# Reordering the first loads of a fused attention and bilinear kernel: key weights in pieces ahead of the second token tile

## The chip, the cores and the metric

The kernel runs on one core of a Trainium2 chip. The metric is device time in microseconds (us), lower being better. Each kernel ran several times. A profile is one execution recorded instruction by instruction; its "span" is some 1.7 us shorter than the time listed for the same execution (1436.2 against 1437.96 us). Times within a profile count from the start of the span.

## The reference, cut to what matters

Four layers run in sequence on x of 2048 tokens by 1024 features: linear attention (A), a bilinear feed-forward block (B), then A and B again with the same weights.

```
x = A_x
x = x + _A_ref(_layernorm(x), A_wqkv, A_wo)              # first the projections q, k of the normalised x
x = x + _B_ref(_layernorm(x), B_w_gate, B_w_up, B_w_down)
x = x + _A_ref(_layernorm(x), A_wqkv, A_wo)
x = x + _B_ref(_layernorm(x), B_w_gate, B_w_up, B_w_down)
```

Only the first microseconds of the first A are changed. A token tile is 128 tokens. It is loaded, normalised, transposed by TensorE so that features lie on partitions, and multiplied by the key weights, 1024 x 1024, in two halves of 512 columns. I number the tiles from one in the text; the code counts from zero.

## The kernel before

Every operation goes through a small planner that records what it reads and writes and derives the semaphore waits from that. The parts that matter here:

```
            def proj(kind, i, h, mid=None):          # tile i, column half h: eight matmuls
                ...
                for ks in ((range(0, 4), range(4, 8)) if mid else (range(KT),)):
                    P.add("pe", ... [e.matmul(psb(bank), xnT[:, k, ...], t[:, k, h * 512:(h + 1) * 512], ...) for k in ks] ...,
                          rd=r_xT(i * 128, (i + 1) * 128) + r_w(base, h * 512, (h + 1) * 512), pwr=[bank])
                    if mid: mid(); mid = None          # something put between the two groups of four
    ...
            lead = [[lambda: lnp.start(2), lambda: lnp.step_t(1)], [lambda: lnp.b_one()], ...]   # after each projection
            #        statistics of tile three, transposes of tile two
    ...
        dma(x_res[:, 0, 0:dh0], ...); dma(x_res[:, 0, dh0:D], ...)    # tile one, two halves
        xload(1)                                                     # tile two
        load_w("k", 0); load_w("k", 1)                               # key weights, 1 MB each
        xload(2); load_w("q", 0); xload(3); load_w("q", 1); xload(4); xload(5)
```

`start` makes a tile's statistics, `b_one` normalises it, and `step_t` makes TensorE transpose it and ScalarE copy the result. All loads are issued by the sync engine (SP).

## Time and profile before

| | before |
|---|---|
| time, median of 3 runs | 1436.02 us (1435.92 to 1436.86) |
| profiled execution, span | 1436.2 us |
| TensorE busy | 1421.7 us, 99% |
| TensorE idle before the first projection | 2.85 us |
| first key half, issued and landed | 2.2 and 9.7 us |
| granted TensorE clock at half | 7.6 to 14.5 us |

A timeline line reads: start, duration, engine, source line, operation, tiles, count, and in brackets the idle time before it with what ended it. The lines themselves are in the prediction.

### The profile page before, as it was taken

The numbers are of one execution on the slowest core, as the hardware profiler recorded it, in microseconds if no ns is written. First come the engines' busy times: TensorE is split into PE (matmuls) and PEld (weight loads), VectorE is DVE, ScalarE is ACT, GpSimd is POOL, SyncE is SP. The second block draws the span as 40 slices with busy tenths as digits, with TensorE's granted clock in tenths as the row PEclk, the third lists the DMA queues.
The fourth block names the chain that finished last, engine by engine and source line by source line (L and its number), as shares of the span: only waits on it lengthen the run. The fifth ranks groups of instructions, "written<-read, shape, count | busy, mean of one in ns | idle before, by whom it ended". The sixth has DMA issues, their size and how long they took to land.

```text
span 1436.2 us, 21761 instructions
## 1 busy us (share of the span) xinstructions
PE 1421.7 (99%) x8110; PEld 787.9 (55%) x8170; DVE 1212.8 (84%) x2377; ACT 677.0 (47%) x1386; POOL 148.5 (10%) x176
## 2 busy tenths in 40 slices
PE   8999999999999999999999999999999999999999
PEld 3444444555545566664544444446666475666547
DVE  6987878999978799988779978778888887888888
ACT  4573355444410266662157824567776004777400
POOL 2202621000010000002000045310000100000000
PEclk9999999999999999999999999999999999999999
DMA  6778978997786777768883266767775976777653
GB/s 195 165 212 224 214 172 195 298 303 267 257 268 203 249 248 251 257 241 286 245 272 109 88 164 158 191 174 262 257 251 192 289 256 224 259 262 256 207 192 120
DMA packets 272570, 320.73 MB, mean 223 GB/s; under 512 B 164048, under 2 KB 214992, under 8 KB 272464
## 3 DMA queue, kind: packets, MB, share of 16 engines
q1 hardware_dynamic: 272464, 319.34, 72.6%
q8 instruction: 64, 1.05, 0.3%
q14 instruction: 42, 0.34, 0.1%
HBM read 236.45 MB, written 73.40 MB: 216 GB/s over the span
## 4 chain that ended last, share of the span: by engine, by line
PE 94%; DVE 4%; issue 1%; ACT 1%; DMA 0%; POOL 0%; DVEq 0%
PE ps L1357 28%; PE ps L1774 17%; PE ps L1438 17%; PE ps L1173 8%; PE ps L1275 7%; PE ps L907 6%; PE ps L939 6%; PE ps L1692 5%; DVE arena L777 2%; DVE arena L452 1%; PE ps L1199 1%; DVE arena L780 0%; PE ps L1226 0%; DVE arena L959 0%; DVE arena L624 0%
## 5 line engine op out<-in xcount | busy, mean ns | idle before, releaser
L777 DVE TENSOR_TENSOR arena<-arena 128x512 f16<-128x512 f16 (+9 forms) x1015 | 497.8, 518 | 59.5 <-ACT arena L1442 34.2
L1357 PE MATMUL ps<-arena 128*128 128x512 f16 x1888 | 457.1, 379 | 1.0 <-DVE arena L780 1.0
L780 DVE SCALAR_TENSOR_TENSOR arena<-ps,arena 128x512 f16<-128x512 f32 (+3 forms) x545 | 353.9, 664 | 68.7 <-PE ps L1774 28.4
L1438 PE MATMUL ps<-arena 128*128 128x256 f16 x2184 | 287.5, 273 | 1.0 <-DVE ps L1451 1.0
L1357 PEld LDWEIGHTS ps<-arena 128*128 128x128 f16 (+1 forms) x1888 | 182.9, 98 | 163.6 <-ACT ps L1386 3.8
L1438 PEld LDWEIGHTS ps<-arena 128*128 128x128 f16 (+1 forms) x2184 | 212.2, 98 | 91.6 <-ACT arena L1442 6.9
L1774 PE MATMUL ps<-arena 128*128 128x512 bf16 (+1 forms) x1102 | 242.6, 379 | 0.9
L1774 PEld LDWEIGHTS ps<-arena 128*128 128x128 f16 x1120 | 109.6, 98 | 130.2
L1362 ACT ACTIVATE arena<-ps 128x512 f32<-128x512 f32 x224 | 133.8, 597 | 76.3 <-PE ps L1357 61.5
L1442 ACT ACTIVATE arena<-ps 128x256 f32<-128x256 f32 x351 | 125.1, 384 | 26.9 <-PE ps L1438 22.0
L939 PE MATMUL ps<-arena 128*128 128x512 f16 (+1 forms) x551 | 122.2, 379 | 1.0 <-ACT arena L946 0.4
L1173 PE MATMUL ps<-arena 128*128 128x512 bf16 x498 | 114.7, 379 | 0.7
L1275 PE MATMUL ps<-arena 128*128 128x512 bf16 x502 | 110.3, 379 | 0.5
L457 POOL TENSOR_SCALAR arena<-arena 128x1 f32<-128x1 f32 x64 | 24.8, 388 | 818.0 <-DVE arena L456 818.0
L1448 ACT COPY ps<-ps 128x256 f32<-128x256 f32 x182 | 66.3, 364 | 74.8 <-DVE arena L780 29.3
L1386 ACT COPY ps<-ps 128x512 f32<-128x512 f32 x112 | 65.4, 584 | 64.4 <-PE ps L1357 52.2
L1041 POOL TENSOR_TENSOR arena<-arena 128x1024 f16<-128x1024 f32 x32 | 77.2, 2412 | 158.3 <-DVE arena L1039 147.8
L452 DVE BATCH_NORM_STATS2 arena<-arena 128x6 f32<-128x512 bf16 x128 | 88.1, 688 | 5.5 <-DMA arena<-in_A_x_dram 3.1
L939 PEld LDWEIGHTS ps<-arena 128*128 128x128 f16 x560 | 54.0, 98 | 68.2 <-ACT arena L946 5.7
L907 PE MATMUL ps<-arena 128*128 128x512 bf16 x375 | 86.1, 385 | 3.6 <-DVE arena L474 2.8
L1692 PE MATMUL ps<-arena 128*128 128x256 f16 (+1 forms) x784 | 86.8, 273 | 0.2 <-ACT ps L1705 0.2
L1451 DVE TENSOR_TENSOR ps<-ps,arena 128x256 f32<-128x256 f32 x182 | 76.7, 428 | 10.5 <-PE ps L1438 9.6
(62 smaller groups left out, 901.3 us busy)
## 6 DMA issues: line engine op xcount, KB each, us to landing
arena<-w_scratch SPq DMA_DIRECT2D x84, 896.0 KB, 4.5
arena<-t_scratch SPq DMA_DIRECT2D x32, 896.0 KB, 6.0
arena<-in_B_w_down_dram SPq DMA_DIRECT2D x24, 896.0 KB, 5.0
arena<-sp_scratch SPq DMA_DIRECT2D x26, 768.0 KB, 4.3
w_scratch<-arena SPq DMA_DIRECT2D x28, 512.0 KB, 6.2
arena<-w_scratch SPq DMA_DIRECT2D x28, 384.0 KB, 5.2
x_scratch<-arena SPq DMA_DIRECT2D x40, 256.0 KB, 7.2
arena<-x_scratch SPq DMA_DIRECT2D x40, 256.0 KB, 5.6
```

The lines of the kernel that those rows point to most:

```text
L777: P.add("dve", lambda e: e.tensor_tensor(out=out, in0=a, in1=b, op=op), rd=rd, wr=wr, prd=prd)
L780: P.add("dve", lambda e: e.scalar_tensor_tensor(out=out, in0=a, scalar=sc, in1=b, op0=ALU.mult, op1=op1), rd=rd, wr=wr, prd=prd)
L907: P.add("pe", (lambda ks: lambda e: [e.matmul(psb(bank), xnT[:, k, i * 128:(i + 1) * 128], t[:, k, h * 512:(h + 1) * 512], start=(k == 0), ...
L939: P.add("pe", lambda e: [e.matmul(psb(bank), a[0][:, k, :], b[0][:, k, :], start=(q in (1, 5) and k == 0), stop=(k == 3), skip_group_check ...
L1173: return [e.matmul(psb(bank), xrt[t][:, jj * 128:(jj + 1) * 128], pk[:, h, t, :], start=(t == tok[0]), stop=(t == tok[NST - 1])) for t in ts]
L1275: return [e.matmul(psb(bank), xnT[:, g, i * 128:(i + 1) * 128], wp[:, g, dh * 512:(dh + 1) * 512], start=(dh == 0 and g == 0), stop=(g == ...
L1357: P.add("pe", lambda e: [e.matmul(psb(bank), w[:, k, :], x[:, k, :], start=(start and k == 0), stop=(k == 3), skip_group_check=True) for k ...
L1362: P.add("act", lambda e: e.activation(t, psb(bank), AF.Copy, scale=SG), prd=[bank], wr=r)
L1438: P.add("pe", lambda e: [e.matmul(psb(bank)[:, 256 * half:256 * half + 256], w[:, k, :], xx[:, k, :], start=(start and k == 0), stop=(k == ...
L1442: P.add("act", lambda e: e.activation(d, src, AF.Copy, scale=sc), prd=[xk], wr=rd_)
L1692: P.add("pe", lambda e: [e.matmul(psb(bank)[:, 256 * half:256 * half + 256], a[:, k, 128 * r:128 * r + 128], b[:, k, :], start=(start and ...
L1774: P.add("pe", lambda e: [e.matmul(psb(bank), hv[:, 7 * hf + k, t * 128:(t + 1) * 128], w[:, k, :], start=(q in "15" and hf == 0 and k == 0 ...
```

## The change

The intent is to start the first projection as soon as tile one is ready: its weights come ahead of tile two, in two pieces of 512 KB, so that the first four matmuls need only the first piece. Tile two's transposes move into the middle of the second projection, since tile two now comes later; tile three's already stood in the middle of the fourth. The diff, cut to its core (the removal of the half-started statistics is left out):

```
-                          rd=r_xT(...) + r_w(base, h * 512, (h + 1) * 512), pwr=[bank])
+                          rd=r_xT(...) + r_w(base, h * 512, (h + 1) * 512)[ks[0]:ks[-1] + 1], pwr=[bank])
...
-                j1 = lnp.start_half()
                 lnp.b_one()
                 lnp.step_t(1)
-                lnp.start_rest(j1)
+                lnp.start(1)
...
+            mids = {("k", 0, 0): lambda: None, ("k", 0, 1): lambda: lnp.step_t(1), ("k", 1, 1): lambda: lnp.step_t(1)}
-            lead = [[lambda: lnp.start(2), lambda: lnp.step_t(1)], ...
+            lead = [[lambda: lnp.start(2)], ...
...
+        for hf in range(2):
+            dma(wk[:, 4 * hf:4 * hf + 4, 0:512], wqkv_v[:, 4 * hf:4 * hf + 4, D:D + 512], ..., (KW["k"][0], KKB)[hf])
         xload(1)
-        load_w("k", 0)
         load_w("k", 1)
```

More of the change, by code (lines that the diff above doesn't have):

```diff
@@ L292, in build_kernel @@
     KXB = dkey("x0b")
+    KKB = dkey("k0b")
     KXS = [dkey("xs%d" % i) for i in range(NST)]
@@ L445, in build_kernel, with ln_a @@
         ln_cnt = [0]
-        def ln_a(i, j=None, hs=(0, 1)):
-            if j is None:
-                j = ln_cnt[0] % 8
-                ln_cnt[0] += 1
-            for h in hs:
+        def ln_a(i):
+            j = ln_cnt[0] % 8
+            ln_cnt[0] += 1
+            for h in range(2):
                 P.add("dve", (lambda h: lambda e: e.bn_stats(st[j][:, 6 * h:6 * h + 6], x_res[:, i, (D // 2) * h:(D // 2) * (h + 1)]))(h),
                       rd=r_x(i, (D // 2) * h, (D // 2) * (h + 1)), wr=R(O_ST[j] + 24 * h, 24))
-            if hs[-1] == 0:
-                return j
             P.add("dve", lambda e: e.bn_aggr(mv[j][:, 0:2], st[j]), rd=R(O_ST[j], 48), wr=R(O_MV[j], 8))
@@ L501, in start @@
                 self.q_b.append((i, j))
-            def start_half(self):
-                return ln_a(self.order[self.n], None, (0,))
-            def start_rest(self, j):
-                ln_a(self.order[self.n], j, (1,))
-                self.q_b.append((self.n, j))
-                self.n += 1
             def b1_one(self):
@@ L908, in proj @@
                                                                 start=(k == 0), stop=(k == KT - 1)) for k in ks])(ks),
-                          rd=r_xT(i * 128, (i + 1) * 128) + r_w(base, h * 512, (h + 1) * 512), pwr=[bank])
+                          rd=r_xT(i * 128, (i + 1) * 128) + r_w(base, h * 512, (h + 1) * 512)[ks[0]:ks[-1] + 1], pwr=[bank])
                     if mid:
@@ L1081, in layer_A @@
             seq += [("q", i) for i in range(max(NPL - NHOLD - 1, 0), NPL if NPL < NST else 0)]
-            lead = [[lambda: lnp.start(2), lambda: lnp.step_t(1)], [lambda: lnp.b_one()], [lambda: lnp.start(3)],
+            mids = {("k", 0, 0): lambda: None, ("k", 0, 1): lambda: lnp.step_t(1), ("k", 1, 1): lambda: lnp.step_t(1)}
+            lead = [[lambda: lnp.start(2)], [lambda: lnp.b_one()], [lambda: lnp.start(3)],
                     [lambda: lnp.b_one()], [], [lambda: lnp.step_t(1)], [lambda: lnp.start(4)], [lambda: lnp.b_one(), lambda: lnp.start(5)]]
@@ L1086, in layer_A @@
                 for h in range(2):
-                    ev = proj(kind, tok[i], h, (lambda: lnp.step_t(1)) if first and (kind, i, h) == ("k", 1, 1) else None)
+                    ev = proj(kind, tok[i], h, mids.pop((kind, i, h), None) if first else None)
                     ev()
@@ L1920, in build_kernel @@
         dma(x_res[:, 0, dh0:D], x2[0:128, dh0:D], r_x(0, dh0, D), KXB)
+        for hf in range(2):
+            dma(wk[:, 4 * hf:4 * hf + 4, 0:512], wqkv_v[:, 4 * hf:4 * hf + 4, D:D + 512], _seg(O_WK + 8 * hf * D, 4, D * 2, 0, 1024), (KW["k"][0], KKB)[hf])
         xload(1)
-        load_w("k", 0)
         load_w("k", 1)
```

## The prediction

Passages whose claims no trace here shows are cut from the prediction, at the marks. Its sum came to -0.2 us (-0.16 + 0.32 - 0.38), hence 1435.8 from 1436.0. The middle term, 0.35 for +0.9, is rival A: half clock once more after the idle time between the first two projections. The +0.9 stands as a guess of mine; the two terms left come to -0.54 us.

Where the prediction speaks of the slowest engine, the trace shows this: each load of the start lands by 16 increments, those of the first key half between 7.30 and 9.66 us, those of the second between 10.28 and 12.65, of which the last came 1.27 us after the one before it (rival B's 1.2 us fits that). That an increment stands for one of the 16 DMA engines that the page counts is my reading. The landing times of part (1) are my estimates, from the place in the queue and the rates of the first profile's stretches (239 to 263 GB/s from 2 to 5 us, 346 to 368 from 5 to 10).

> **What bounds the kernel now.** I read the page first, then the granted clock in stretches of one microsecond, then the first 25 us engine by engine, because the diff touches nothing that runs later.
>
> ```profile
> PE 1421.7 (99%) x8110; PEld 787.9 (55%) x8170; DVE 1212.8 (84%) x2377; ACT 677.0 (47%) x1386; POOL 148.5 (10%) x176
> ...
> PE 94%; DVE 4%; issue 1%; ACT 1%; DMA 0%; POOL 0%; DVEq 0%
> ```
>
> The first line is busy time by engine, the second the chain that ended last. TensorE is busy for 1421.7 of 1436.2 us, so all its idle time together is 14.5 us, and it carries 94% of the chain. A microsecond taken off before its first dense stretch should come off the end, since every later stage is paced by TensorE; a change that only reorders the start has at most the idle and slow time of the start to win. How much that is, the timeline of TensorE shows (start, duration, line, count, then the idle time and its releaser):
>
> ```profile
> 1.36 3.73 PE L431 MATMUL ps<-arena 128*128 128x512 f16 x10 [1.36 <-POOL arena L427]
> 6.33 0.62 PE L557 MATMUL ps<-arena 128*128 128x128 f16 x8 [1.24 <-DVE arena L474]
> 9.79 3.57 PE L907 MATMUL ps<-arena 128*128 128x512 bf16 x8 [2.85 <-DVE arena L474]
> 13.16 1.06 PE L565 MATMUL ps<-arena 128*128 128x128 f16 x8
> 14.01 4.71 PE L907 MATMUL ps<-arena 128*128 128x512 bf16 x19
> 18.56 0.61 PE L565 MATMUL ps<-arena 128*128 128x128 f16 x8
> 19.00 1.03 PE L907 MATMUL ps<-arena 128*128 128x512 bf16 x4
> 20.27 1.90 PE L907 MATMUL ps<-arena 128*128 128x512 bf16 x8 [0.24 <-ACT arena L567]
> ```
>
> Ten warm-up matmuls, the transposes of token tile one (L557), an idle gap of 2.85 us, the first key projection (L907, eight matmuls for 512 columns), the transposes of tile two (L565), then nearly gapless work. The gap is put down to a vector instruction, the normalisation of tile two (L474), but the code has no such dependency: the first projection needs tile one's transposed copy, whose last part ends at 7.40, and the first key weights. The sync engine's queue and the landing of single transfers tell which is late:
>
> ```profile
> 0.79 1.35 SPq L424 DMA_DIRECT2D arena<-in_A_x_dram  x3
> 2.18 1.06 SPq L424 DMA_DIRECT2D arena<-in_A_wqkv_dram  x2
> 3.28 2.38 SPq L424 DMA_DIRECT2D arena<-in_A_x_dram  x1
> ```
>
> ```profile
> DMA to landing us min/median/max: 7.5/7.5/7.5
> ...
> DMA to landing us min/median/max: 10.0/10.0/10.0
> ```
>
> The last two are the first and second half of the key weights, by columns (1 MB each). They were issued at 2.18 and about 2.7, so they landed near **9.7** and **12.7**. The first projection starts at 9.79: it waits for the weights. Token tile two, issued at 1.7 with 2.8 us to landing, was there at 4.5 and is used only from 7.3 or so. It sits in the queue ahead of something needed sooner; that is the case for the change.
>
> ```profile
> 6.00:7.00 1.00, 0.62 (x8) 0.45 (x8) 0.29 (x2) 0.24 (x1) 0.00 (x0) 1.00 1.04 346
> 7.00:8.00 1.00, 0.00 (x0) 0.00 (x0) 1.00 (x2) 0.35 (x1) 0.00 (x0) 0.82 1.06 368
> 9.00:10.00 1.00, 0.21 (x1) 0.14 (x2) 0.55 (x1) 0.00 (x0) 0.22 (x1) 0.50 1.10 356
> 14.00:15.00 1.00, 1.00 (x7) 0.47 (x5) 0.71 (x3) 1.00 (x2) 0.00 (x0) 0.77 1.08 365
> ```
>
> These are stretches of the start; the last three columns are granted clock, share of the DMA engines, GB/s. The clock falls to half at about 7.64 (0.82 of the microsecond from 7 to 8) and comes back at about 14.46 (0.77 of that from 14 to 15). The eight first matmuls therefore start about 0.43 us apart; later ones need (4.71/19 and less) about 0.22. The queue is saturated: some 355 GB/s from 5 us on.
>
> [...] at 9.7 us the queue had moved 24+263+239+260+350+346+368+361+0.7x356 = 2460 KB, though x tile one, x tile two and the first key half are only 1573 KB. The slowest engine is thus about 0.9 MB of total traffic, or 2.5 us, behind. [...]
>
> **The change part by part.**
> (1) Load order. Before: tile one, tile two, key half one, key half two. After: tile one, key half one in two pieces of 512 KB by rows, tile two, key half two. I scale landing by position. Before the end of the first piece stand 786 KB; at 300 KB per us after tile one (first tile down by 3.5) that is 5 to 5.5 for a typical engine, up to 7 for the slowest. The second piece ends at 1311 KB: 262 KB less than before, at 355 KB/us 0.75 us earlier, near 8.9. Tile two moves to the place where the first key half ended, 1573 KB: 9.7 instead of 4.5. Key half two has the same 2621 KB up to its end and should land where it did, at **12.7**. One more issue on the sync engine costs about 0.45 us of its time, while the queue holds over 1 MB: hidden.
> (2) First projection in two parts of four matmuls. The first can start at about 7.45, when the transposed copy is there. Mostly at half clock, eight need 8 x 0.427 = 3.4: it ends near 10.8, the second piece having come at 8.9. Before it ended near 13.2. That is 2.4 us sooner, but not yet a gain: the second projection needs key half two.
> (3) Tile two's vector chain starts on landing: two statistics of 0.71, aggregate 0.22, two small pool steps 0.23 and 0.58, normalisation 0.56, with 0.3 of hand-overs, 2.6 us. From 9.7 it ends at 12.3 to 12.5. Moving its transposes from before to the middle of the second projection leaves them room until about 13.6. No loss.
> (4) Second projection, from 12.75. At full clock: four matmuls 0.86, transposes 0.45, four matmuls 0.86, end near 14.9. The third projection needs the copy of the transposes by ScalarE, 1.02 us (L567) plus some 0.2 to start, against four matmuls of cover: like the gap of 0.24 that the timeline has at 20.27, some 0.3 to 0.4 us are lost. It starts at 15.3. Before: 14.01 plus 8 x 0.217, at 15.75. **Sum: 15.75 - 15.3 = 0.4 us won**, out of 2.4 hoped for. The third tile's chain is not later than before: its transposes came at 18.34 with its normalisation done at 18.24, and here the vector work in front of it moves forward by about as much.
> (5) The removal of the half-started statistics moves 0.7 us of vector work that had nothing waiting on it: zero.
>
> **The rivals.**
> Rival A, the clock. After the first projection ends at 10.8, TensorE idles until 12.75 and then works through the gap. [...]
> Rival B, the landing. If the slowest engine lagged because of tile two's early load or how the loads met, the order may shrink that lag; a second engine's worth, 1.2 us, would put key half two at 11.5, and the gain at 1.5 us. In favour: the rate is only 239 to 263 GB/s from 2 to 5 us, where tile two runs. [...]
> Rival C, the full intent: the 2.4 us of the first projection are kept. It needs key half two by 10.8, for which nothing in the queue speaks.
>
> **Range and chances.** Weights 0.4 for -0.4, 0.35 for +0.9, 0.25 for -1.5: -0.16 + 0.32 - 0.38 = -0.2. From 1436.0 this is **1435.8 us**. The three runs of before lie 0.9 us apart[...], so I widen the rivals' extremes only a little: **1434.0 to 1437.6**. Two per cent are 28.7 us, more than the whole of TensorE's idle time: 0.98 for within 2%, 0.01 for either side.
>
> **What would show it.** First L907 matmul at 7.4 to 7.6, eight of them by 9.2 to 10.9; a new gap before the second group of projections that ends at 12.6 to 12.9; key half two landing at 12.7; tile two landing near 9.7, its normalisation at 12.3 to 12.5; a wait of 0.2 to 0.5 us on L567 before the third projection. Half clock between 14 and 18 us shows rival A. A second projection before 12 us shows rival B. I would be wrong about the kind of effect if the end moved by over 3 us, or if the first projection still waited past 9 us for its second piece.

## The result, and the profile after

| | before | after |
|---|---|---|
| time, median | 1435.97 us, 4 runs (1434.81 to 1436.86) | 1436.74 us, 4 runs (1436.02 to 1437.78) |
| span of the profiled execution | 1436.2 us | 1434.8 us |

The ratio is 1.0006, with a 95% interval of 0.9989 to 1.0024: the same, within the predicted range. A ratio here is the mean time of one kernel's runs over that of the other's of the same rounds, so it is not quite the ratio of the medians. The profiled executions point the other way from the medians, and that is the first lesson: single executions of one kernel differ by more than the change does.

The start of the kernel after, TensorE's timeline:

```profile
6.92 0.62 PE L547 MATMUL ps<-arena 128*128 128x128 f16 x8 [1.58 <-DVE arena L472]
8.06 4.46 PE L897 MATMUL ps<-arena 128*128 128x512 bf16 x12 [0.52 <-DVE arena L549]
12.35 0.61 PE L555 MATMUL ps<-arena 128*128 128x128 f16 x8
12.80 1.03 PE L897 MATMUL ps<-arena 128*128 128x512 bf16 x4
14.07 2.76 PE L897 MATMUL ps<-arena 128*128 128x512 bf16 x11 [0.24 <-ACT arena L557]
...
18.38 3.63 PE L897 MATMUL ps<-arena 128*128 128x512 bf16 x16 [0.24 <-ACT arena L557]
```

L547 and L555 are the transposes of tile one and of the later tiles, L897 the projections, L557 ScalarE's copy of the transposes. The first projection starts at 8.06 instead of 9.79. It and the first four matmuls of the second run without a gap, the third projection starts at 14.07, and the fifth at 18.38, where before it started at 20.27: a lead of 1.9 us. The transposes of tile one came late, at 6.92 instead of 6.33, because the second half of tile one landed at 4.3 instead of 3.5. The clock is granted in full again from 11.5 us (again stretches, with the clock the third number from the end):

```profile
10.00:11.00 1.00, 1.00 (x4) 0.29 (x2) 0.12 (x1) 0.00 (x0) 0.71 (x2) 0.50 1.07 369
11.00:12.00 1.00, 1.00 (x5) 0.31 (x4) 0.55 (x1) 0.34 (x1) 0.08 (x1) 0.73 1.07 354
```

The sync engine's queue, and the time to landing of the last key half:

```profile
1.70 0.98 SPq L425 DMA_DIRECT2D arena<-in_A_wqkv_dram  x2
2.73 0.50 SPq L425 DMA_DIRECT2D arena<-in_A_x_dram  x1
3.27 0.43 SPq L425 DMA_DIRECT2D arena<-in_A_wqkv_dram  x1
```

```profile
DMA to landing us min/median/max: 8.1/8.1/8.1
```

3.27 plus 8.1 is 11.4: the second key half landed 1.2 us sooner (11.41 against 12.65 by the trace) than in the profile of before, though the same bytes stand ahead of it. I come back to that with the control.

The lead of 1.9 us does not reach the end. The spans differ by 1.4 us. Matching instructions of the two traces, the lead is 1.89 us up to 190 us, about 2.1 from 230 to 1120 us, and 1.43 after. The place of the loss is one wait of VectorE, near the start of the last layer, for a transposing transfer (a DMA transpose within the on-chip memory). First before, then after:

```profile
1126.58 0.55 DVE L474 TENSOR_SCALAR arena<-arena 128x1024 f16<-128x1024 bf16 x1 [3.99 <-DMA arena<-arena]
```

```profile
1125.15 0.55 DVE L472 TENSOR_SCALAR arena<-arena 128x1024 f16<-128x1024 bf16 x1 [4.66 <-DMA arena<-arena]
```

The wait is 0.67 us longer after, just the drop from 2.1 to 1.43. Nothing in the diff is near it.

### The profile page after: what moved, and what is told of

It is laid out like the page before. It is cut to its first block, busy times and chain, and to the rows that moved or that the text cites. A ratio compares the mean times of both kernels' runs of the same rounds, so it can differ in the third digit from the quotient of the medians.

```text
span 1434.8 us, 21762 instructions
## 1 busy us (share of the span) xinstructions
PE 1421.6 (99%) x8110; PEld 787.2 (55%) x8170; DVE 1213.4 (85%) x2377; ACT 676.7 (47%) x1386; POOL 148.2 (10%) x176
## 4 chain that ended last, share of the span: by engine, by line
PE 91%; DVE 5%; issue 1%; ACT 1%; DMA 1%; SPq 0%; POOL 0%; POOLq 0%; DVEq 0%
PE ps L1347 28%; PE ps L1428 17%; PE ps L1764 14%; PE ps L1265 8%; PE ps L1163 8%; PE ps L897 6%; PE ps L929 5%; PE ps L1682 5%; DVE arena L767 3%; DVE arena L770 1%; DMA arena<-arena 1%; PE ps L1189 1%; PE ps L1216 0%; DVE arena L949 0%; DVE arena L452 0%
## 5 line engine op out<-in xcount | busy, mean ns | idle before, releaser
L897 PE MATMUL ps<-arena 128*128 128x512 bf16 x375 | 86.1, 384 | 1.5 <-DVE arena L549 0.5
```

The costliest lines, as they stand in the source:

```text
L897: P.add("pe", (lambda ks: lambda e: [e.matmul(psb(bank), xnT[:, k, i * 128:(i + 1) * 128], t[:, k, h * 512:(h + 1) * 512], start=(k == 0), ...
```

## The experiments

Twelve kernels ran, three calls of three or four kernels and one call of a single kernel, each with five rounds. Kernels of one call share a chip and the runs of the kernel before.

### The two kernels again: before_again and after_again

No edit. 

> Control: the kernel before, unchanged. Theory (the change moves only the first 20 us, and the rest of the program follows rigidly[...]): ratio 1.000, and its own runs spread by about 1 to 2 us. Its profile gives a second sample of the start: if the first key half lands again near 9.7 us, the lag of the slowest engine belongs to the load order; if it lands at 8 to 9, it belongs to the execution. Rival (the change costs 0.8 us somewhere that the two profiles do not show): this control is nearer 1435.9 and clearly below the kernel after.

> The kernel after, unchanged, on the same chip and in the same rounds as the control. Theory: within 2 us of the control, ratio 0.9985 to 1.0007, and the start of its third projection (14.07 in the first profile) between 13.9 and 16. If the start is reproducibly earlier by 1.5 to 2 us, the ratio should be near 0.9988. Rival: the change is a wash [...]; then the third projection starts later than 15.5 in this profile or the clock is at half between 12 and 18 us.

Measured in the same rounds: before_again 1435.63 us (ratio 1.0001), after_again 1436.41 us (ratio 1.0003, interval 0.9990 to 1.0017). The nine runs of the kernel before went from 1433.91 to 1438.47, a spread of 4.6 us, where 1 to 2 had been expected. The third projection of after_again starts at 13.57 us, a little before the expected 13.9 to 16, and that of the control at 13.66: it is not reproducibly earlier. The start of before_again:

```profile
6.25 0.62 PE L557 MATMUL ps<-arena 128*128 128x128 f16 x8 [1.05 <-DVE arena L474]
8.20 3.38 PE L907 MATMUL ps<-arena 128*128 128x512 bf16 x8 [1.33 <-DVE arena L456]
11.42 0.61 PE L565 MATMUL ps<-arena 128*128 128x128 f16 x8
...
18.21 3.63 PE L907 MATMUL ps<-arena 128*128 128x512 bf16 x16 [0.24 <-ACT arena L567]
```

Then the start of after_again:

```profile
7.33 1.90 PE L897 MATMUL ps<-arena 128*128 128x512 bf16 x8 [0.52 <-DVE arena L549]
10.98 1.04 PE L897 MATMUL ps<-arena 128*128 128x512 bf16 x4 [1.76 <-DMA arena<-in_A_wqkv_dram]
11.86 0.61 PE L555 MATMUL ps<-arena 128*128 128x128 f16 x8
...
17.89 3.63 PE L897 MATMUL ps<-arena 128*128 128x512 bf16 x16 [0.24 <-ACT arena L557]
```

The unchanged kernel reached its fifth projection at 18.21 instead of 20.27, 2.1 us earlier than itself. So most of the 1.9 us between the first two profiles belongs to the executions. What differed is how late the last of a load's 16 increments came, by my reading the slowest DMA engine: in the first profile of before, the first key half's increments came between 7.30 and 9.66 us, in the control between 7.27 and 8.07. The first is the same to 0.03 us; the last moved by 1.6.

In after_again the bound lies open: with the eight matmuls in 1.90 us (and the clock at 1.00 in the stretches from 9 us on), they are done at 9.2, and TensorE then stands idle for 1.76 us until the second key half has landed at 10.94. The wait is named in the line. That gives a better measure than any start time, the distance from this landing to the start of the fifth projection (landing by the trace; all in us):

| execution | second key half landed | fifth projection | distance |
|---|---|---|---|
| before | 12.65 | 20.27 | 7.6 |
| before_again | 11.07 | 18.21 | 7.1 |
| before_extra_issue (below) | 12.34 | 19.38 | 7.0 |
| before_36_waits (below) | 11.56 | 19.45 | 7.9 |
| after | 11.41 | 18.38 | 7.0 |
| after_again | 10.94 | 17.89 | 7.0 |
| after_merged_load (below) | 11.09 | 18.04 | 7.0 |

With the landing taken out, the change is worth between 0.1 us and 0.65 us at the start (0.9 against before_36_waits, where the clock stayed at half until 13.9 us).

Two cautions. In the kernel before, the second projection does not wait for this landing: in the first three executions it starts at 14.01, 11.87 and 13.03, which is 0.7 to 1.4 us later, after the first projection and tile two's transposes. What it follows there is the first key half, which landed 3.0 us before the second in each of these executions, so the distance still compares like with like. And taking the landing out also takes out what the new order may do to the landing itself. In the five profiles with the loads of before (before_clock_held, 11.92, is the fifth) the second half landed at 11.1 to 12.7 us, 11.9 on average; in the four with the new order and a whole second half (order_t_between, 11.20, is the fourth) at 10.9 to 11.4, 11.2 on average. These ranges overlap, so an effect of the order on the landing is neither shown nor excluded.

### The load order without moving the transposes: order_t_between

```
-  mids = {..., ("k", 0, 1): lambda: lnp.step_t(1), ...};  lead = [[lambda: lnp.start(2)], ...
+  mids = {..., ("k", 0, 1): lambda: None, ...};           lead = [[lambda: lnp.start(2), lambda: lnp.step_t(1)], ...
```

> The change without the move of tile two's transposes: they stand before the second projection again, the loads are as in the kernel after. Theory: tile two lands near 8.4 to 9.7, its normalisation ends 3.1 us later, at 11.7 to 12.8, and the second projection cannot start before the transposes are through. Against the kernel after, the second projection starts 0.4 to 1 us later but the 0.24 us wait for the copy of the transposes goes, so the third projection starts 0 to 0.5 us later; in the time at most 0.5 us, not resolvable. Rival: the move of the transposes is worth as much as the load order; then 1 us or more is lost.

Measured: 1437.32 us, ratio 1.0007 (0.9995 to 1.0020), not to be told from the kernel after by time. Its timeline and stretches:

```profile
7.43 1.90 PE L897 MATMUL ps<-arena 128*128 128x512 bf16 x8 [0.52 <-DVE arena L549]
11.52 1.03 PE L555 MATMUL ps<-arena 128*128 128x128 f16 x8 [2.19 <-DVE arena L472]
12.35 5.70 PE L897 MATMUL ps<-arena 128*128 128x512 bf16 x19
...
19.60 1.69 PE L897 MATMUL ps<-arena 128*128 128x512 bf16 x7 [0.24 <-ACT arena L557]
```

```profile
11.00:12.00 1.00, 0.48 (x5) 0.48 (x6) 0.96 (x3) 0.00 (x0) 0.00 (x0) 0.70 1.10 359
12.00:13.00 1.00, 1.00 (x8) 0.66 (x6) 0.96 (x3) 0.40 (x1) 0.00 (x0) 0.50 1.09 347
```

TensorE idled 2.19 us for tile two's normalisation, and at 11.4 us the clock fell to half, until 14.8. Most of the second projection ran at half clock; the third starts at 15.30, which is 1.2 to 1.7 us later than in the two profiles of the kernel after, where 0 to 0.5 had been expected. The distance from the second key half (landed at 11.20) to the fifth projection is 8.4 instead of 7.0. This is the prediction's rival A, in an execution of a kernel that differs from the kernel after only in where tile two's transposes stand. One execution shows that it happens; how often, it doesn't.

### The halves without the load order: halves_tile_first

```
+  xload(1)                       # tile two second again
   for hf in range(2): dma(wk[:, 4 * hf:4 * hf + 4, 0:512], ...)
-  xload(1)
```

> The change without the reorder: tile two is loaded second again, the first key weights still in two pieces and the transposes in the middle. Theory: the first piece lands about 0.75 us later than in the kernel after (262 KB at 355 KB/us) and so does the second, the second key half at the same 11.4 to 12.7; since the second key half is what the second projection waits for, the third projection starts within 0.5 us of the kernel after's. The halves, not the order, then make the first start earlier. Rival: the order itself matters for the slowest engine; then the first key pieces have all landed only after 9 us and the third projection starts over 1 us later than in the kernel after.

Measured: 1437.24 us, ratio 1.0009 (0.9997 to 1.0022). The second key half landed at 11.74 and the fifth projection started at 18.69: a distance of 6.95 us, as in the kernel after. The third projection started at 14.37, 0.3 and 0.8 us after those of the two profiles of the kernel after. So, by this one profile, as long as the second key half comes whole, the position of tile two is worth nothing measurable at the start; the pieces and the moved transposes do as well with tile two loaded second. The rival's mark, the last piece of the first key half landing only after 9 us, was not reached: it landed at 8.8.

### One sync-engine instruction more or less: before_extra_issue and after_merged_load

The two profiles of the kernel after both lose time at the late wait (4.66 and 5.31 us) against 3.99 and 4.06 in the two of the kernel before. In both of the former, an 8 KB fetch of instructions, which the profile lists as a DMA queue of its own (q14 instruction: 42 packets, 0.34 MB), starts between the landing of the last token load and the landing of the transposing transfer. The change adds one transfer, so from then on each of the sync engine's instructions stands one place further on. These two kernels test that.

```
# before_extra_issue: tile six's load cut in two
-  xload(5)
+  dma(x_res[:, 5, 0:dh0], ...); dma(x_res[:, 5, dh0:D], ...)
# after_merged_load: tiles five and six in one transfer
-  xload(4); xload(5)
+  dma(x_res[:, 4:6, :], x2[512:768, :].rearrange("(i p) d -> p i d", p=128), r_x(4) + r_x(5), KX[4])
```

> The kernel before with tile six's load cut in two halves: one more transfer for the sync engine, at a place where nothing waits for it. Theory (instruction count): the wait near 1120 us grows from 4.0 to 4.6 us or more, and the fetch of instructions falls inside it, without any change of the start. Rival (the load order or chance): the wait stays near 4.0 us.

> The kernel after, with token tiles five and six loaded by one transfer instead of two, so that the sync engine has as many instructions as in the kernel before. In the two profiles of the kernel after, VectorE waits 4.66 and 5.31 us for a transposing transfer near 1120 us, in the two of the kernel before 3.99 and 4.06; an 8 KB fetch of instructions starts inside that wait only in the former. Theory: the added transfer shifts the sync engine's instructions by one and moves that fetch ahead of the transposing transfer, which costs about 0.6 us; with the count restored the fetch is after the wait again, the wait is 4.0 to 4.2 us, and the ratio falls by some 0.0004 against the kernel after. Rival: the longer wait is chance or comes from the load order through the state of the DMA engines; it stays at 4.6 us or more.

The wait itself also contains the lateness of the eight token loads ahead of it (the last of them landed at 1123.32 us in after_again and at 1122.62 in before_again), so I take the distance between two landings: last token load, then transposing transfer. For the kernel before, the two are issued at 1119.5 and 1120.0:

```profile
DMA to landing us min/median/max: 5.9/5.9/5.9
...
DMA to landing us min/median/max: 6.5/6.5/6.5
```

They land at 1125.4 and 1126.5. For the kernel after, issued at 1117.4 and 1117.9:

```profile
DMA to landing us min/median/max: 6.0/6.0/6.0
...
DMA to landing us min/median/max: 7.2/7.2/7.2
```

They land at 1123.4 and 1125.1. Between those two landings, the DMA queues of the kernel after hold one packet of the instruction queue, and in the kernel before's there is none (queue, packets, MB, share):

```profile
q14 instruction: 1, 0.01, 1.5%
```

By the trace, to two decimals, in all fourteen profiles:

| execution | fetch inside | last load to transposing transfer |
|---|---|---|
| before, before_again | no | 1.03, 1.13 |
| before_extra_issue | yes | 1.62 |
| after, after_again | yes | 1.65, 1.66 |
| order_t_between, halves_tile_first | yes | 1.66, 1.70 |
| after_merged_load | no | 1.12 |
| before_clock_held, split_and_clock, before_36_waits (below) | no | 1.01, 1.03, 1.15 |
| second_split_aligned, tile_between_halves, second_split_again (below) | no | 1.09, 1.09, 0.95 |

One added instruction in the kernel before brings the longer time, one removed from the kernel after takes it away. The fetch in the way costs about **0.55 us**. In the times it cannot be seen: before_extra_issue 1436.27 us (ratio 0.9999), after_merged_load 1436.16 us (1.0003), with intervals of some 0.0013 to either side. By the wait, the picture is less clean. before_extra_issue waited 4.76 us, as expected. But after_merged_load waited 5.74 us in all, where the last increments of most of the token loads came some 2 us after the first. My expectation (a wait of 4.0 to 4.2) failed, and by the mark set beforehand (4.6 or more) this run spoke for the rival; the distance from load to transposing transfer, which speaks for the theory, I chose afterwards. Of the 1.25 us by which after_again waits longer than before_again, too, only 0.5 are the fetch; the other 0.7 are a later landing of the last load (1123.32 against 1122.62).

### Keeping the clock up: before_clock_held and split_and_clock

```
+  def keep_clock(n):                                # n matmuls of 512 columns on zeros, result unused
+      P.add("pe", lambda e: [e.matmul(psb(B_KVT[1]), wrm[:, 0:128], wrm, start=True, stop=True) for _ in range(n)], ...)
# before_clock_held: PE_WARM 10 -> 16, and keep_clock(12) after the transposes of tile one
# split_and_clock:   PE_WARM 10 -> 18, keep_clock(3) there, keep_clock(2) after the first projection,
#                    and the second key half in two pieces like the first
```

> The kernel before, with matmuls on zeros keeping TensorE busy: 16 instead of 10 warm-up matmuls and 12 more between the transposes of tile one and the first projection. Theory: the clock stays full over the first projection, which then needs 8 x 0.217 = 1.7 us instead of 3.4; what follows is bounded by the second key half (landings 11.1 to 12.7 in the two profiles), so of 1.7 us saved some 0.5 to 1.3 remain: the third projection starts 0.5 to 1.3 us earlier than in a profile with the same landing, and the ratio is 0.9991 to 0.9997. Rival: half clock costs its full 1.7 to 2 us; ratio 0.9986 or less. Rival two: the added matmuls delay the transposes and nothing is won.

> The kernel after with the second key half also loaded in two pieces, 18 warm-up matmuls and short runs of matmuls on zeros between the transposes and the first projection and after the first projection. Theory: the wait for the whole second key half is the step that bounds the start of the kernel after (landing 11.41 and 10.94, second projection at 11.4 and 10.98); its first piece lands some 1.4 us before, at 9.6 to 10.1, and the clock stays full, so the second projection starts near 10 and the third, which then needs the copy of tile two's transposes (normalisation 11.1 to 11.7, transposes 0.6, copy 1.0), near 13.0 to 13.4 instead of 13.6 to 14.1: 0.5 to 1 us won. Rival: the second projection does not start before 11 us, so the landing of the second half was not the bound.

Measured: before_clock_held 1438.46 us, ratio **1.0016** (1.0004 to 1.0029), slower by an interval clear of 1; split_and_clock 1437.55 us, ratio 1.0007 (0.9995 to 1.0020). The start of before_clock_held did what was wanted in part: full clock from 6.3 us on, the first projection in 1.89 us, the distance from the second key half to the fifth projection 6.9 us, with a lead of 1.46 us over the first profile of before. Half of that lead is an earlier landing (11.92 against 12.65). And the twelve added matmuls were still running when the first key weights landed at 8.93, so the first projection began only at 10.29. The third projection starts 2.3 us after the second key half's landing, against 2.5 to 3.3 in before, before_again and before_extra_issue: 0.2 to 1.0 us won, where 0.5 to 1.3 had been expected. But by 228 us the lead is gone, at another wait of VectorE for a transposing transfer. Before, then before_clock_held:

```profile
227.65 1.23 DVE L777 TENSOR_TENSOR arena<-arena 128x2048 f16<-128x2048 f16 x1 [3.38 <-DMA arena<-arena]
```

```profile
227.68 1.23 DVE L781 TENSOR_TENSOR arena<-arena 128x2048 f16<-128x2048 f16 x1 [4.87 <-DMA arena<-arena]
```

In before_clock_held a 16 KB fetch of instructions, of another queue, starts at 224.8 us, 0.4 us before one transposing transfer lands (225.2), and the next lands only at 227.7; in the kernel before that fetch starts at 230.1. The lead falls there from 1.6 us to nothing. This does not account for the whole difference in time, some 2.3 us by the ratio: the profile's span is only 0.5 us longer than that of the first profile of before, which was itself a long execution (1437.96 us). The rest stays open. split_and_clock, which adds 13 matmuls instead of 18, shows the same: fetch at 225.0, wait 4.27 us. Its start did not go as expected either: 18 warm-up matmuls, which took 6.49 us (0.36 us each, against 0.24 in the first projection behind them), pushed the transposes of tile one to 7.69 us, the second projection started at 10.99 where near 10 was expected, and the third at 13.67, not at 13.0 to 13.4.

### The added instructions without the matmuls: before_36_waits

```
+  [e.wait_ge(esem["pool"], 1) for _ in range(3)]    # ahead of each of the first twelve groups of projections, long satisfied
```

> The kernel before with 36 instructions added to TensorE's stream that do nothing: waits, three ahead of each of the first twelve groups of projections, for a semaphore value reached long before. Clock, loads and matmuls are as before. In the kernel with the clock held, which has 18 more matmuls with their 18 weight loads, VectorE waits 4.87 us for a transposing transfer near 227 us, against 2.6 to 3.4 in the kernels before and after. Theory: 36 added instructions move one of TensorE's 16 KB fetches of instructions from about 228.5 to 225, between the transposing transfers, and that costs about 1.5 us; it will be seen here too, wait 4.2 us or more, ratio near 1.001. Rival: the long wait is chance, or comes from the added matmuls; then it stays at 2.6 to 3.4 us.

Measured: 1437.69 us, ratio 1.0010 (0.9997 to 1.0022). The trace lists 20 more instructions than that of before (21781 against 21761), not 36; why, it does not show. The wait, and the fetch in the queues between 225.4 and 228.3 us:

```profile
228.34 1.23 DVE L777 TENSOR_TENSOR arena<-arena 128x2048 f16<-128x2048 f16 x1 [4.62 <-DMA arena<-arena]
```

```profile
q8 instruction: 1, 0.02, 3.2%
```

The fetch starts at 225.9, and the transposing transfers land at 225.4 and 228.3, 2.9 us apart; in the kernel before they are 1.0 apart (226.67 and 227.63). With matmuls and loads untouched, the idle instructions bring the longer wait (4.62 us against 3.38), and the added matmuls themselves are not needed for it. The traces do not say for which engine a fetch is; that this one is TensorE's, as the expectation has it, is my reading of its move from 230.1 to 225.9 us when TensorE's stream alone was lengthened. In the three executions with the fetch there (before_clock_held, split_and_clock, before_36_waits) the two landings are 2.4 to 2.9 us apart, against 0.9 to 1.3 in the other eleven: about **1.4 to 1.9 us** more than in before. A fetch close to a landing does not always cost: in after_merged_load one of 16 KB starts at 226.6, between this transfer's landing (226.1) and the next one's (227.3), and these are 1.2 us apart, no more than the 1.3 in before, where no fetch falls between them. That the fetch delays the transfer, and is not just a mark of something else that moves with it, I take from the three pairs (before_extra_issue and before_36_waits against before, after_merged_load against after) in which little but the instruction count differs; the traces do not name the DMA engine that a packet runs on.

### A version that might beat both: second_split_aligned, tile_between_halves, second_split_again

If the landing of the whole second key half bounds the start, it should come in two pieces as well. The sync engine's instruction count is put back by loading tiles five to seven in one transfer.

```
-  load_w("k", 1)
+  for hf in range(2): dma(wk[:, 4 * hf:4 * hf + 4, 512:1024], ..., (KW["k"][1], KKC)[hf])
-  xload(4); xload(5)                  # and tile seven later
+  dma(x_res[:, 4:7, :], x2[512:896, :].rearrange("(i p) d -> p i d", p=128), ..., KX[4])
# tile_between_halves also: xload(1) between the two pieces of the first key half
```

> The kernel after with the second key half loaded in two pieces as well, no added matmuls, and tiles five to seven loaded by one transfer, so that the sync engine's instruction count is that of the kernel before from there on. In all profiles of kernels with the new load order the fifth projection starts 6.95 us after the second key half has landed (18.38 less 11.41, 17.89 less 10.94), which says that this landing is the bound. Theory: with its first piece usable 1.5 us sooner, the second projection starts before the second piece has landed, and the next bound is tile two: landing near 8.1 to 8.4, chain 3.2, transposes 0.6, copy 1.0, third projection near 13.2, fifth near 17.5; that is 6.2 to 6.5 us after the landing of the last piece, some 0.5 won. The wait near 1120 us is free of the instruction fetch. Rival: no gain, the distance stays 6.9 or more.

> As the last, but token tile two is loaded between the two pieces of the first key half, so it lands some 1.5 us earlier. Theory: tile two's chain then ends near 10 and no longer bounds the third projection; the second projection's second part waits for the last key piece (11.1 or later) and the third starts about 1.1 us after that landing: fifth projection 5.6 to 6.0 us after the landing of the last piece, about 1 us less than in the kernel after. In the time this is 0.0007, within the noise of five rounds. Rival: the first projection's second piece, now 0.75 us later, holds everything back, and the distance is 6.5 or more.

Measured: second_split_aligned 1435.25 us, ratio 0.9996 (0.9984 to 1.0009); tile_between_halves 1435.88 us, ratio 1.0001 (0.9987 to 1.0015). The start of second_split_aligned:

```profile
7.43 1.90 PE L898 MATMUL ps<-arena 128*128 128x512 bf16 x8 [0.52 <-DVE arena L550]
10.06 1.04 PE L898 MATMUL ps<-arena 128*128 128x512 bf16 x4 [0.72 <-DMA arena<-in_A_wqkv_dram]
11.80 0.62 PE L556 MATMUL ps<-arena 128*128 128x128 f16 x8 [0.71 <-DVE arena L473]
```

The second projection starts at 10.06, 1.4 us before the last piece has landed (11.49), and then waits for tile two's normalisation, as expected. The distance to the fifth projection is 17.84 - 11.49 = 6.35 us, against 6.95 ("all profiles" in the expectation leaves out order_t_between, which had 8.4): 0.6 won, which shows that the landing of the whole half was the bound of the kernel after. With tile two ahead of the second piece it is 17.96 - 12.19 = 5.8, another 0.6. The late wait is 3.84 us, the transposing transfer 1.1 us behind the last load.

> The aligned kernel with both key halves in pieces once more, unchanged, to see whether its lead of five rounds (median 1435.25 against 1436.24, ratio 0.9996) is more than noise. Theory: some 0.1 to 0.6 us from the landing of the second half, 0.6 from the second bound removed, nothing lost to instruction fetches: ratio 0.9992 to 0.9999 again, and in the profile a wait near 1120 us of about 1.1 us after the last token load, a fifth projection 6.2 to 6.5 us after the last key piece. Rival (noise): ratio 1.0000 or above.

Measured: 1436.26 us, ratio 1.0001 (0.9987 to 1.0014), with a distance of 17.23 - 11.11 = 6.1 us at the start. The lead of the first five rounds was noise, or is too small to hold against it. None of these versions is shown to beat the kernel before.

## Why the prediction was right or wrong

**The time.** 1436.74 us lies in the range, and "the same" was right. The reason given held: all that the change touches is a few microseconds of a start, and what it removes was waiting for something that it is not shown to bring sooner. That the median fell into the range is in part luck, though: the range is 3.6 us wide, the nine runs of the unchanged kernel spread over 4.6 us, and the range was drawn from three runs that lay 0.9 us apart. No time measured here can tell the predicted gain of 0.2 us from the 0.8 us by which the median is longer.

**The bound by the second key half** was the step that mattered, and it was right. In after_again TensorE waits for that landing by name, the distance from it to the fifth projection is 7.0 us in every execution of the kernel after and 7.0 to 7.6 in those of before, and splitting that half shortens it. It bounds the kernel after, as predicted. The predicted gain of 0.4 us lies within the 0.1 to 0.65 that remain when the landing is taken out. Its sum has a slip: it starts the third projection of before at 15.75, with all eight matmuls at full clock, but the first ones still ran at half clock and the trace has 15.97, so that the sum should have been some 0.7. The wait for ScalarE's copy was there too: 0.24 us before the third projection.

**The landing times** were mis-sized: "Key half two has the same 2621 KB up to its end and should land where it did, at 12.7". It landed at 11.41 and 10.94. The order of the bytes was right, but I took the 2.5 us lag of the slowest engine in one profile for a property of the load order. The control landed it at 11.07 in the unchanged order. The lag of the slowest engine behind the fastest (last increment behind the first), for this half, was 2.4 us in the first profile and 0.8 in the control, and 1.3 and 0.6 in the two of after. Rival B asked whether the new order shrinks that lag. The control shows that a small lag comes in the old order too; over all profiles it is 0.8 to 2.4 us in the old order (five) and 0.6 to 1.3 in the new (four, second half whole), so rival B is not excluded. Its sign, a second projection before 12 us, came in both profiles of the kernel after (11.46 and 10.98), but also in before_again (11.87), so it can't decide.

**The first projection** began at 8.06 and 7.33 against 7.4 to 7.6 expected; the later one because tile one's second half came late. The new gap before the second projection was seen in after_again (1.76 us), and not in the first profile, where half clock filled it.

**Tile two's chain** takes 3.2 us from landing to the end of its normalisation (8.43 to 11.67), not the 2.6 that the prediction gives. The terms were right and the sum was not: 1.42, 0.22, 0.81, 0.56 and 0.3 make 3.3. Tile two landed at 8.4 and not at 9.7, another landing put too late, and that hid the error: luck. That tile two was "used only from 7.3" before is not quite so either: the half-started statistics ran on it at 4.64 us, but nothing waited for them.

**Rival A, half clock after the idle time,** came in neither profile of the kernel after. It came in order_t_between, where the idle time was 2.19 us in place of the 1.76 of after_again (clock 0.50 from 12 to 14 us, against 1.00). What sets the clock back is not shown.

**"A microsecond taken off before its first dense stretch should come off the end"** failed as a sum. Leads do pass rigidly through hundreds of microseconds (about 2.1 us from 230 to 1120 us), but the change also adds one instruction to the sync engine, and the place of an instruction fetch that this moves costs 0.55 us near 1120 us. By the profiles, that takes back most or all of the gain of 0.1 to 0.65; the times can't resolve it. No rival of mine had it.

## What to carry to other kernels

Before explaining a difference of a microsecond between two profiles, profile the unchanged kernel again: here it differed from itself at the start by more than the change was worth. Measure from the event that bounds the stretch (here a landing), and not from time zero. And when a local gain does not arrive at the end, follow the lead along the two traces to the wait where it drops: adding a transfer or a few instructions can move an instruction fetch into a transfer that the kernel waits for (here 0.55 us near 1120 us, and 1.4 to 1.9 us near 226).
